# GFNet plus ReGLU on one core: half-height passes of the last 36 units in nine runs of eight, with the transforms' PSUM pair lent to the fourth unit

## The chip, the core and the metric

The kernel runs on one core of one Trainium2 chip. The metric is device time in microseconds (us) of one execution, shown as the median over several runs. The core has a matrix engine (TensorE, PE in the profile, with its weight loads as PEld), a vector engine (VectorE, DVE), a scalar engine (ScalarE, ACT), GpSimd (POOL) and SyncE (SP), which issues the transfers (its queue is SPq). Matmul results land in PSUM, which this kernel divides into eight banks of 128 partitions x 512 fp32 values.

## The reference

The output is the sum of the input, a two-dimensional Fourier filter (GFNet) of its layernorm, and a ReGLU MLP of the same layernorm. S = 2048 rows, D = 448 columns, F = 1792 hidden columns, everything fp32:

```
xn = layernorm(x)                                    # x: 2048 x 448
A  = irfft2(rfft2(xn) * (w_r + 1j * w_i), s=(S, D))  # w: 2048 x 225
g  = xn @ W_gate                                     # 448 x 1792
g  = g * (g > 0)
B  = (g * (xn @ W_up)) @ W_down                      # W_down: 1792 x 448
return x + A + B
```

## The kernel before

**MLP.** The rows are held transposed in four chunks of 512 (`CHUNKS`, index `q`, tiles `T`), the hidden columns in 14 slices of 128 (index `f`), in three groups of 5, 5 and 4 slices (`GROUPS`). One **unit** is one `f` for one `q`; there are 56. Every operand is split into a high and a low fp16 part, and three of the four products are kept. D = 448 is three and a half rows of 128, so a unit needs, for gate and for up each, ten full-height passes (`gu_full`, L757: 128 contraction rows, 512 columns) and one **half-height** pass (`gu_half`, L764: 64 rows). Gate and up of a unit each fill one PSUM bank. ScalarE then takes the ReLU of the gate (`gu_relu`, L799), VectorE multiplies by the up (`gu_times`, L803), and both split the product into fp16 halves `h` (`gu_hi`, L807; `gu_lo`, L811). These four are `gu_post`. When all units of a group are there for a chunk, four down passes (`dn_mm`, L834) of 12 or 15 matmuls each follow, and VectorE adds each result to the running output `xy` (`dn_post`, L840). The last four down passes of all are `dn_tail` (L853 matmuls, L857 VectorE), the last of them in two pieces of 336 and 112 columns.

**Runs of half passes.** Units are taken in sets: four sets of two, then sixteen of three. The first unit of a set does its full passes, and then the half passes of the whole set stand together (`gu_halves`), since changing between full and half height costs TensorE time. The other units of the set open their banks with their half pass; their full passes follow later.

**PSUM.** Six of the eight banks are three pairs for the units and the down passes (`banks`; those without an owner are in the list `idle`). The other two are a rotating pool tile `fx` with two buffers, for the transforms' matmuls.

**Transforms.** The Fourier work is a chain of small steps: `f_dft`, `f_eo`, `f_x`, `f_sdft`, `f_y1` forward, butterflies on VectorE, the filter, and then inverse. Per block of 128 rows (`n2`, sixteen) the inverse has the mirror-and-add steps `i_pair` and `i_quad` (with a transfer of mirrored rows, `sw`), `i_hi` (L632, ScalarE) and `i_lo` (L638, VectorE), `i_sdft` (L648, TensorE, 12 matmuls into `fx`), `i_pq` (L653, ScalarE) and `i_pqlo` (L657, VectorE), which read that bank, `i_ddft` (L667, TensorE, 12 matmuls into `fx`) and `i_acc` (L672, VectorE), which reads it. A single real row goes its own way (`row_dft` L593, `row_mul`, `row_ev`).

**Order.** The steps of the transforms stand in one list (`bg`), each with a VectorE cost, and a planner (`rooms`, `load`) gives each unit and each down pass a share of them. The program is recorded unit by unit, with priorities (`tc.high_priority`); a scheduler then fixes one order per engine. Each engine works through its own order and waits at an instruction whose inputs or bank are not ready.

Of the kernel before, what the change touches and what calls it, by code (L numbers as in the profile page):

```python
# [1 line left out]

# [18 lines left out]
GW = 2 * KC  # L21
# [3 lines left out]
LAG, AHEAD, RAMP = 1, 5, 8  # L25
NWARM = 21
# [118 lines left out]
def tile_gfnet_reglu(ctx: ExitStack, tc: tile.TileContext, x, xr, xi, wgu, wd, wf, c_fd, c_fm, c_im, c_row, c_id,  # L145
# [9 lines left out]

    def fx():
        return psum.tile([128, 512], F32, name="fx", bufs=2)
# [201 lines left out]
    zps, eo, X, Xh, yps, cur = {}, {}, {}, {}, {}, {}  # L359

    def f_dft(n2):
        q, j = n2 % 4, n2 // 4
        js = slice(128 * j, 128 * (j + 1))
        ps = fx()
        T = Tq[q]

        def mm(r, a, part, first=False):
            o = fd_off[part, r]
            P.matmul(ps[:, r * GW:(r + 1) * GW], T[:, a, js] if a < 8 else Tl[q][:, js], fd_t[:, o:o + GW],  # L369
                     start=first, stop=True, skip_group_check=True)  # L370
# [6 lines left out]
        zps[n2] = ps  # L377

    def f_eo(n2):
        ps = zps[n2]  # L380
        zc = ft([128, 2 * GW], F32, "zc", 2)
        A.activation(zc, ps[:, 2 * GW:4 * GW], AF.Copy, scale=2.0 ** -14)
# [3 lines left out]
        V.scalar_tensor_tensor(e2[:, 2 * GW:], ps[:, 0:2 * GW], 2.0 ** -14, zc, op0=OP.mult, op1=OP.subtract)  # L386
# [254 lines left out]
    def i_sdft(n2):  # L641
# [7 lines left out]
        sps[n2] = ps  # L649

    def i_pq(n2):
        pgh[n2] = it([GW, 2, 4, 128], F16, "pgh", 2)
        A.activation(pgh[n2][:, 0].rearrange("p a b -> p (a b)"), sps[n2][0:GW], AF.Copy, scale=2.0 ** -14)  # L653

    def i_pqlo(n2):
        hi, lo = (pgh[n2][:, h].rearrange("p a b -> p (a b)") for h in range(2))
        V.scalar_tensor_tensor(lo, sps[n2][0:GW], 2.0 ** -14, hi, op0=OP.mult, op1=OP.subtract)  # L657
# [3 lines left out]
    def i_ddft(n2):  # L661
# [7 lines left out]
        ips[n2] = ps  # L669

    def i_acc(n2):
        V.scalar_tensor_tensor(xy[:, n2, :], ips[n2][:, 0:D], fsc[:, 1:2], xy[:, n2, :], op0=OP.mult, op1=OP.add)  # L672
        store(n2)
# [94 lines left out]

    NOSYNC = mybir.DependencyInfo(mybir.DependencyClass.NoSync, mybir.DependencyReason.DATA)
    opened = set()  # L770

    def gu_unit(f, q, others):
# [22 lines left out]
    g1s = {}  # L795

# [415 lines left out]
    for i, u in list(enumerate(units))[START + 1:-4]:  # L1212
# [78 lines left out]
```

## Time and profile before

| | |
|---|---|
| time, median of 3 runs | 442.37 us (442.14 to 443.46) |
| the profiled execution | 443.54 us |
| its span, first to last instruction | 441.8 us |
| granted TensorE clock | 1.000 |
| busy PE | 435.3 us (99%) |
| busy DVE | 382.4 us (87%) |
| busy ACT | 184.6 us (42%) |
| busy POOL | 29.0 us (7%) |

In the rows of the profile, `L757` is a line of the kernel, `out<-in` the tiles by the program's names, and the shape that of one instruction. In a timeline a row has its start in us, its length, engine, line, operation and count (`x29`); instructions of one form that follow each other share a row. What ended an engine's idle time before the row stands in square brackets with its length. A matmul's own duration includes its way through the array, so that matmuls overlap; the cost of one is the pitch from start to start.

### The profile page before, as it was taken

The numbers are of one execution on the slowest core, as the hardware profiler recorded it, in microseconds if no ns is written. First come the engines' busy times: TensorE is split into PE (matmuls) and PEld (weight loads), VectorE is DVE, ScalarE is ACT, GpSimd is POOL, SyncE is SP. The second block draws the span as 40 slices with busy tenths as digits, with TensorE's granted clock in tenths as the row PEclk, the third lists the DMA queues.
The fourth block names the chain that finished last, engine by engine and source line by source line (L and its number), as shares of the span: only waits on it lengthen the run. The fifth ranks groups of instructions, "written<-read, shape, count | busy, mean of one in ns | idle before, by whom it ended". The sixth has DMA issues, their size and how long they took to land.

```text
span 441.8 us, 7428 instructions
## 1 busy us (share of the span) xinstructions
PE 435.3 (99%) x2641; PEld 221.5 (50%) x2641; DVE 382.4 (87%) x957; ACT 184.6 (42%) x396; POOL 29.0 (7%) x75
## 2 busy tenths in 40 slices
PE   8999999999999999999999999999999999999997
PEld 3743454454555544444545444444545556555664
DVE  6998677788996879999999999988997989798644
ACT  5995454274557327144023358233213232244220
POOL 3230020011100040000000020000000000000000
PEclk9999999999999999999999999999999999999999
DMA  7929899004021124242220210001111121210212
GB/s 244 322 75 213 267 357 216 23 1 97 23 86 58 45 68 129 84 127 85 85 85 1 84 42 2 0 1 42 43 43 49 48 98 30 74 56 33 77 63 104
DMA packets 37612, 39.54 MB, mean 90 GB/s; under 512 B 16534, under 2 KB 33352, under 8 KB 37576
## 3 DMA queue, kind: packets, MB, share of 16 engines
q1 hardware_dynamic: 37576, 39.09, 29.3%
q8 instruction: 20, 0.33, 0.3%
q14 instruction: 16, 0.13, 0.1%
HBM read 24.38 MB, written 3.67 MB: 64 GB/s over the span
## 4 chain that ended last, share of the span: by engine, by line
PE 90%; ACT 3%; DVE 2%; DMA 2%; issue 1%; SPq 1%; POOL 0%; ACTq 0%
PE bank L757 49%; PE bank L834 27%; PE bank L764 3%; PE fx L648 2%; PE fx L369 2%; PE fx L667 2%; PE fx L406 2%; PE bank L853 2%; DMA y<-in_xr 1%; DMA T<-tt 1%; ACT wt L699 1%; ACT junk L185 1%; ACT tt L304 1%; DVE wt L703 1%; DVE g L803 0%
## 5 line engine op out<-in xcount | busy, mean ns | idle before, releaser
L757 PE MATMUL bank<-T,wt 128*128 128x512 f16 (+1 forms) x1160 | 253.2, 372 | 1.8 <-DMA T<-tt 1.1
L757 PEld LDWEIGHTS <-wt 128*128 128x128 f16 x1160 | 110.9, 98 | 128.4 <-issue 7.2
L834 PE MATMUL bank<-wdt,h 128*128 128x448 f16 x624 | 122.6, 352 | 0.0
L834 PEld LDWEIGHTS <-h 128*128 128x128 f16 x624 | 60.6, 98 | 55.4
L807 ACT ACTIVATE h<-g 128x512 f16<-128x512 f32 x56 | 35.0, 627 | 77.2 <-DVE g L803 77.2
L799 ACT ACTIVATE g<-bank 128x512 f32<-128x512 f32 x56 | 33.2, 592 | 79.9 <-PE bank L757 43.8
L803 DVE SCALAR_TENSOR_TENSOR g<-bank,g 128x512 f32<-128x512 f32 x56 | 38.4, 685 | 10.8 <-PE bank L757 7.0
L811 DVE TENSOR_TENSOR h<-g,h 128x512 f16<-128x512 f32 x56 | 38.4, 686 | 10.3 <-ACT h L807 10.2
L840 DVE SCALAR_TENSOR_TENSOR xy<-bank,dsc,xy 128x448 f32<-128x448 f32 x44 | 29.9, 679 | 3.2 <-PE bank L834 2.9
L632 ACT ACTIVATE vt<-y,fsc 128x456 f16<-128x456 f32 x15 | 10.1, 674 | 34.5 <-issue 14.0
L699 ACT ACTIVATE wt<-wst,wsc 128x512 f16<-128x512 f32 x28 | 19.3, 714 | 11.7 <-DVE wsc L195 10.0
L703 DVE SCALAR_TENSOR_TENSOR wt<-wst,wsc,wt 128x512 f16<-128x512 f32 x28 | 20.4, 743 | 0.5 <-ACT wt L699 0.5
L188 POOL PARTITION_ALL_REDUCE wm<-wm x15 | 10.3, 686 | 152.1 <-ACT junk L185 117.6
L672 DVE SCALAR_TENSOR_TENSOR xy<-fx,fsc,xy 128x448 f32<-128x448 f32 x16 | 10.8, 681 | 10.9 <-PE fx L667 10.9
L185 ACT ACTIVATE junk<-wst 128x512 bf16<-128x512 f32 x28 | 17.2, 616 | 0.0
L764 PE MATMUL bank<-T,wt 64*128 64x512 f16 x112 | 15.6, 380 | 0.0
L397 ACT ACTIVATE Xh<-X 128x456 f16<-128x456 f32 x16 | 9.3, 579 | 13.0 <-DVE X L395 8.3
L648 PE MATMUL fx<-im,vt 128*128 128x128 f16 x192 | 13.3, 219 | 0.0
L667 PEld LDWEIGHTS <-pgh 114*128 114x128 f16 x192 | 10.9, 98 | 3.8 <-issue 0.8
L406 PE MATMUL fx<-Xh,fm 128*128 128x456 f16 x48 | 12.7, 356 | 0.0
L648 PEld LDWEIGHTS <-vt 128*128 128x128 f16 x192 | 11.6, 98 | 1.3
L667 PE MATMUL fx<-idc_t,pgh 114*128 114x112 f16 x192 | 12.1, 213 | 0.0
(168 smaller groups left out, 478.3 us busy)
## 6 DMA issues: line engine op xcount, KB each, us to landing
wst<-in_wgu SPq DMA_DIRECT2D x28, 256.0 KB
sw<-y SPq DMA_DIRECT2D x56, 112.2 KB
wf<-in_wf SPq DMA_DIRECT2D x16, 228.0 KB
xy<-in_x SPq DMA_DIRECT2D x16, 224.0 KB
y<-in_xr SPq DMA_DIRECT2D x15, 224.0 KB
out<-xy SPq DMA_DIRECT2D x15, 224.0 KB
wdst<-in_wd SPq DMA_DIRECT2D x14, 224.0 KB
fm<-in_c_fm SPq DMA_DIRECT2D x4, 256.0 KB
```

Of the source, the lines that this page charges most:

```text
L648: P.matmul(o, v[:, h, w], m[:, c, :], start=(i == 0), stop=(i == 2), skip_group_check=True)
L667: P.matmul(ps[:, o], h[:, a, i, :], idc_t[:, b, o], start=(j == 0), stop=(j == 2), skip_group_check=True)
L699: A.activation(w[:, 0:4, :], wst[f, g], AF.Copy, scale=wsc[f, g])
L703: V.scalar_tensor_tensor(w[:, 4:8, :], st, sc, w[:, 0:4, :], op0=OP.mult, op1=OP.subtract)
L757: last["P"] = P.matmul(hps[f, q][g][:, cs], wt[f, g][:, a, :], Tq[q][:, b, cs], start=(start and i == 0), stop=(stop and i == len(seq) - 1 ...
L764: m = P.matmul(hps[f, q][g][:, 0:512], wt[f, g][rows, 7, :], Tq[q][rows, b, :], start=start, stop=stop).ins
L799: last["A"] = A.activation(g1s[f, q], hps[f, q][0], AF.Relu, scale=2.0 ** -22).ins
L803: last["V"] = V.scalar_tensor_tensor(g1, hps[f, q][1], 2.0 ** -22, g1, op0=OP.mult, op1=OP.mult).ins
L807: A.activation(ht[f, q][:, 0, :], g1s[f, q], AF.Copy)
L811: V.tensor_tensor(h[:, 1, :], g1s.pop((f, q)), h[:, 0, :], op=OP.subtract)
L834: last["P"] = P.matmul(ps[:, 0:D], ht[f, q][:, a, js], wdt[f][:, b, :], start=(i == 0), stop=(i == n - 1)).ins
L840: last["V"] = V.scalar_tensor_tensor(xy[:, n2, :], dps[n2][:, 0:D], dsc[:, g:g + 1], xy[:, n2, :], op0=OP.mult, op1=OP.add).ins
```

## The change

The sets are four of two, four of three and nine of four (`RUNS`), so that the last 36 units' half passes stand in nine runs of eight where there were twelve of six. A set of four needs four bank pairs at once. The fourth is the transforms' pair: `fx` is no longer a rotating pool tile but two fixed banks, kept in `turn["pair"]`, which `fx()` takes in turn. In a run of eight one unit, for which no pair is idle, gets this pair. Its half passes come first in the run, and the first of them waits for the recorded readers of the pair (`seen`). The unit that closes with the run (the one whose full passes came before it) is read out at once (`gu_post` within `gu_halves`), and its pair becomes the transforms' pair. Before the set's first unit, `read_all` issues with a high priority all readers of the pair that are still outstanding (`f_eo`, `f_y1`, `row_mul`, `row_ev`, `i_pq`, `i_pqlo`, `i_acc`, each now issued once, by whoever comes first). Pending down passes now come before the last unit of a set rather than before its second. The number of matmuls of each kind and of the other engines' operations stays.

The diff, cut: the same bookkeeping of readers (`seen["fx"].append`, `reads`, `@reader`) is added to all functions named above and shown here for two of them.

```diff
+READ = 600
+RUNS = 4 * [3] + 9 * [4]
...
+    turn = {"pair": [psum.tile([128, 512], F32, name=f"fx{i}") for i in range(2)], "n": 0}
+
     def fx():
-        return psum.tile([128, 512], F32, name="fx", bufs=2)
+        turn["n"] += 1
+        return turn["pair"][turn["n"] % 2]
...
+    seen = {"fx": []}
+    unread, read = {}, set()
+
+    def reads(name, *fns):
+
+        for fn in fns:
+            unread[fn.__name__, name] = fn
+
+    def reader(fn):
+        @wraps(fn)
+        def once(*a):
+            key = fn.__name__, a
+            if key not in read:
+                read.add(key)
+                unread.pop(key, None)
+                fn(*a)
+        return once
+
+    def read_all():
+        for (_, a), fn in list(unread.items()):
+            fn(*a)
...
         sps[n2] = ps
-
+        reads((n2,), i_pq, i_pqlo)
+
...
+    @reader
     def i_pqlo(n2):
         hi, lo = (pgh[n2][:, h].rearrange("p a b -> p (a b)") for h in range(2))
-        V.scalar_tensor_tensor(lo, sps[n2][0:GW], 2.0 ** -14, hi, op0=OP.mult, op1=OP.subtract)
+        seen["fx"].append(V.scalar_tensor_tensor(lo, sps[n2][0:GW], 2.0 ** -14, hi, op0=OP.mult, op1=OP.subtract).ins)
...
         gu_open(f, q)
+        if len(others) > 2:
+            with tc.high_priority(offset=READ):
+                read_all()
         gu_full(f, q, gs, cs, True, False)
         gu_halves(f, q, *others)
...
         fresh = [u for u in others if u not in hps]
         for u in fresh:
-            gu_open(*u)
-        for i, u in enumerate((*others[::-1], (f, q))):
+            if idle:
+                gu_open(*u)
+            else:
+                hps[u] = turn["pair"]
+        lent = [u for u in fresh if hps[u] is turn["pair"]]
+        wait = seen["fx"] + [r for u in fresh for r in seen.get(id(hps[u]), [])] if lent else []
+        if lent:
+            seen["fx"] = []
+        order = lent + [u for u in (*others[::-1], (f, q)) if u not in lent]
+        for i, u in enumerate(order):
             for g in (1, 0):
                 with tc.high_priority(offset=2000 if i or not g else 0):
-                    m = gu_half(*u, g, u in fresh, m, i == len(others))
+                    m = gu_half(*u, g, u in fresh, m, u == (f, q))
+                    for r in wait:
+                        tc.add_manual_dep(m, r.name, SYNC, reason="half passes stand together")
+                    wait = []
         opened.update(others)
         gu_close(f, q)
+        if lent:
+            with tc.high_priority(offset=400):
+                gu_post(f, q)
+            posted.add((f, q))
+            turn["pair"] = idle.pop()
...
-    sets += [gseq[k:k + 3] for k in range(8, len(gseq), 3)]
+    k = 8
+    for n in RUNS:
+        sets.append(gseq[k:k + n])
+        k += n
...
-            if u == us[1] and pend and len(units) > START:
+            if u == us[-2 if len(us) > 2 else 1] and pend and len(units) > START:
...
-            with tc.high_priority(offset=400):
-                gu_post(f, q)
+            if (f, q) not in posted:
+                with tc.high_priority(offset=400):
+                    gu_post(f, q)
```

Functions move to other lines: `gu_full` from L757 to L796, `gu_half` from L764 to L803, `gu_relu` L799 to L859, `gu_times` L803 to L863, `gu_lo` L811 to L871, `i_sdft` L648 to L682, `i_pqlo` L657 to L694, `i_ddft` L667 to L704, `i_acc` L672 to L711, `i_lo` L638 to L672, `dn_tail` L853 and L857 to L915 and L919.

The order of instructions at three places follows, with the weight loads mostly left out; a row names the result's tile, its sources, and the semaphores that it waits for. First TensorE at the last run of half passes; `im` is the matrix of `i_sdft`, `T3` the transposed rows of the last chunk. Before:

```order
L667 MATMUL fx_4388<-idc_t_83,pgh_4275 128x112
L648 MATMUL fx_4401<-im_4193,vt1_2151 128x128 [waits PE_49]
...
L757 MATMUL bank2_113<-T3_65,wt_3117 128x512
...
L757 MATMUL bank3_114<-T3_65,wt_3120 128x512
...
L764 MATMUL bank1_112<-T3_65,wt_3305 128x512 [waits DVE_49]
L764 MATMUL bank0_111<-T3_65,wt_3302 128x512 [waits Activation_49]
L764 MATMUL bank5_116<-T3_65,wt_3249 128x512
L764 MATMUL bank4_115<-T3_65,wt_3246 128x512
L764 MATMUL bank3_114<-T3_65,wt_3120 128x512
L764 MATMUL bank2_113<-T3_65,wt_3117 128x512
```

And with the change:

```order
L682 MATMUL fx1_62<-im_4051,vt0_2122 128x128 [waits DVE_49]
...
L796 MATMUL bank3_116<-T3_67,wt_3035 128x512
...
L803 LDWEIGHTS wt_3174 [waits DVE_49]
L803 MATMUL fx1_62<-T3_67,wt_3174 128x512
...
L803 MATMUL fx0_61<-T3_67,wt_3171 128x512
...
L803 MATMUL bank1_114<-T3_67,wt_3127 128x512
...
L803 MATMUL bank0_113<-T3_67,wt_3124 128x512
...
L803 MATMUL bank3_116<-T3_67,wt_3035 128x512
...
L803 MATMUL bank2_115<-T3_67,wt_3032 128x512
```

Before, twelve `i_sdft` matmuls are followed by 14 full passes and a run of six into the three pairs. Now they are followed by eight full passes of the same unit and a run of eight, which starts in the bank (`fx1_62`) that the `i_sdft` has just written; the wait on VectorE stands on the weight load ahead of the first half pass.

That wait is for `i_pqlo` (L694) of this `i_sdft`. What VectorE has ahead of it with the change, from the multiply of the unit before on (`y3`, `y6`, `y7`, `y8` are blocks on their way through `i_pair` and `i_quad`; `sw2` holds mirrored rows):

```order
L863 SCALAR_TENSOR_TENSOR g1_4301<-bank1_114,g1_4301 128x512 [waits PE_49,Activation_49]
...
L711 SCALAR_TENSOR_TENSOR xy_63<-fx0_61,fsc_89,xy_63 128x448 [waits PE_49]
...
L655 TENSOR_TENSOR y7_75<-y7_75 128x228 [waits DVE_49]
L871 TENSOR_TENSOR h_4304<-g1_4301,h_4304 128x512 [waits Activation_49]
...
L584 TENSOR_TENSOR y6_74<-y6_74,sw2_2130 128x4x57 [waits DMAHW4_49,DMAHW3_49,DMAHW2_49]
L585 TENSOR_TENSOR y6_74<-y6_74,sw2_2130 128x4x57
...
L672 SCALAR_TENSOR_TENSOR vt0_2122<-y8_76,fsc_89,vt0_2122 128x456 [waits PE_49,Activation_49]
L694 SCALAR_TENSOR_TENSOR pgh_4297<-fx1_62,pgh_4297 114x512 [waits Activation_49]
```

Between that multiply and L694 stand thirteen operations. The last of them, L672, is the `i_lo` of a later block; it writes `vt0`, which this `i_sdft` reads, so it can't start ahead of that transform's end.

Last the end of TensorE's order. Before, and with the change:

```order
L667 MATMUL fx_4740<-idc_t_83,pgh_4706 128x112 [waits DVE_49]
...
L667 MATMUL fx_4754<-idc_t_83,pgh_4737 128x112 [waits DVE_49]
...
L853 MATMUL bank0_111<-wdt_3382,h_4430 128x336
...
L853 MATMUL fx_4824<-wdt_3382,h_4430 128x112 [waits DVE_49]
```

```order
L915 MATMUL fx0_61<-wdt_3387,h_4338 128x336
...
L704 MATMUL bank2_115<-idc_t_85,pgh_4643 128x112 [waits DVE_49]
...
L704 MATMUL bank3_116<-idc_t_85,pgh_4672 128x112 [waits DVE_49]
...
L915 MATMUL bank2_115<-wdt_3387,h_4338 128x112 [waits DVE_49]
```

The last two `i_ddft` (12 matmuls each) have moved from ahead of the 336-column piece to behind it, and the 112-column piece now shares its bank with the first of them. On VectorE the five operations at the end were L672, L672, L857 (448 columns), L857 (336), L857 (112) before, and are L711, L711, L919 (448), L919 (336), L919 (112) now.

More of the change, by code (lines that the diff above doesn't have):

```diff
@@ L1 @@
 from contextlib import ExitStack, contextmanager
+from functools import wraps
 import numpy as np
@@ L377, in f_dft @@
         zps[n2] = ps
+        reads((n2,), f_eo)
+    @reader
     def f_eo(n2):
@@ L381, in f_eo @@
         zc = ft([128, 2 * GW], F32, "zc", 2)
-        A.activation(zc, ps[:, 2 * GW:4 * GW], AF.Copy, scale=2.0 ** -14)
+        seen["fx"].append(A.activation(zc, ps[:, 2 * GW:4 * GW], AF.Copy, scale=2.0 ** -14).ins)
         e = eo[n2] = ft([128, 4, 2, KC], F32, "eo", 2)
@@ L385, in f_eo @@
         V.scalar_tensor_tensor(e2[:, 0:2 * GW], ps[:, 0:2 * GW], 2.0 ** -14, zc, op0=OP.mult, op1=OP.add)
-        V.scalar_tensor_tensor(e2[:, 2 * GW:], ps[:, 0:2 * GW], 2.0 ** -14, zc, op0=OP.mult, op1=OP.subtract)
+        seen["fx"].append(V.scalar_tensor_tensor(e2[:, 2 * GW:], ps[:, 0:2 * GW], 2.0 ** -14, zc, op0=OP.mult, op1=OP.subtract).ins)
     def f_x(n2):
@@ L406, in f_sdft @@
             P.matmul(y, m[:, a, :], xh[:, b], start=(i == 0), stop=(i == 2), skip_group_check=True)
+        reads((n2,), f_y1)
     def fresh(other):
@@ L444, in bfly @@
         return t, u
+    @reader
     def f_y1(n2):
@@ L448, in f_y1 @@
         if n2 < 8:
-            A.activation(t, yps[n2], AF.Copy)
+            seen["fx"].append(A.activation(t, yps[n2], AF.Copy).ins)
             cur["y", n2] = t
@@ L454, in f_y1 @@
             V.tensor_tensor(t, a, ps, op=OP.add)
-            V.tensor_tensor(u, a, ps, op=OP.subtract)
+            seen["fx"].append(V.tensor_tensor(u, a, ps, op=OP.subtract).ins)
             cur["s1", n2 - 8, 0], cur["s1", n2 - 8, 1] = t, u
@@ L593, in row_dft @@
             P.matmul(y, row_t[:, d, a], state["rowh"], start=(a == 0), stop=(a == 1), skip_group_check=True)
+        reads((), (row_mul, row_ev)[d])
+    @reader
     def row_mul():
@@ L601, in row_mul @@
         V.tensor_tensor(v, v, t, op=OP.add)
+    @reader
     def row_ev():
@@ L649, in i_sdft @@
         sps[n2] = ps
+        reads((n2,), i_pq, i_pqlo)
+    @reader
     def i_pq(n2):
         pgh[n2] = it([GW, 2, 4, 128], F16, "pgh", 2)
-        A.activation(pgh[n2][:, 0].rearrange("p a b -> p (a b)"), sps[n2][0:GW], AF.Copy, scale=2.0 ** -14)
+        seen["fx"].append(A.activation(pgh[n2][:, 0].rearrange("p a b -> p (a b)"), sps[n2][0:GW], AF.Copy, scale=2.0 ** -14).ins)
+    @reader
     def i_pqlo(n2):
         hi, lo = (pgh[n2][:, h].rearrange("p a b -> p (a b)") for h in range(2))
-        V.scalar_tensor_tensor(lo, sps[n2][0:GW], 2.0 ** -14, hi, op0=OP.mult, op1=OP.subtract)
+        seen["fx"].append(V.scalar_tensor_tensor(lo, sps[n2][0:GW], 2.0 ** -14, hi, op0=OP.mult, op1=OP.subtract).ins)
     ips = {}
@@ L669, in i_ddft @@
         ips[n2] = ps
+        reads((n2,), i_acc)
+    @reader
     def i_acc(n2):
-        V.scalar_tensor_tensor(xy[:, n2, :], ips[n2][:, 0:D], fsc[:, 1:2], xy[:, n2, :], op0=OP.mult, op1=OP.add)
+        seen["fx"].append(V.scalar_tensor_tensor(xy[:, n2, :], ips[n2][:, 0:D], fsc[:, 1:2], xy[:, n2, :], op0=OP.mult, op1=OP.add).ins)
         store(n2)
@@ L767, in gu_half @@
         return m
+    SYNC = mybir.DependencyInfo(mybir.DependencyClass.Sync, mybir.DependencyReason.DATA)
     NOSYNC = mybir.DependencyInfo(mybir.DependencyClass.NoSync, mybir.DependencyReason.DATA)
@@ L815, in gu_post @@
         gu_times(f, q)
+        seen[id(hps[f, q])] = [last["A"], last["V"]]
         gu_hi(f, q)
@@ L841, in dn_post @@
                                            op0=OP.mult, op1=OP.add).ins
+        seen[id(state["dn"])] = [last["V"]]
     def dn_tail(fs, ns):
```

1 line of the change is left out of this document (added).

## The prediction

> **What bounds the kernel now.** I read the page first, then who waited for whom on TensorE, then the timeline around single runs of half-height passes, and last the timeline of the end. Of the page:
>
> ```profile
> span 441.8 us, 7428 instructions
> ...
> PE 435.3 (99%) x2641; PEld 221.5 (50%) x2641; DVE 382.4 (87%) x957; ACT 184.6 (42%) x396; POOL 29.0 (7%) x75
> ```
>
> TensorE is busy for 435.3 of 441.8 us. A busy row alone proves little, so I asked what TensorE waited for after its first 40 us, and how busy the engines are in the middle (columns: PE, PEld, DVE, ACT, POOL, clock, DMA):
>
> ```profile
> PE bank L757 <- DMA T<-tt: 1.1, 1, 1.1
> ...
> 160.00:300.00 140.00, 140.00 (x696) 64.85 (x695) 136.00 (x318) 54.26 (x134) 9.95 (x19) 1.00 0.21 62
> ```
>
> One wait of 1.1 us is all. So what is taken out of TensorE's stream is gained in full, and a new wait in it is lost in full. VectorE is second, with 136.00 of 140 us between 160 and 300.
>
> **What a run costs, and what three fewer save.** The timeline (start, length, engine, line, count) around a run of six, and a run of four:
>
> ```profile
> 299.63 6.42 PE L757 MATMUL bank<-T,wt 128*128 128x512 f16 x29
> 305.98 0.82 PE L764 MATMUL bank<-T,wt 64*128 64x512 f16 x6
> 306.73 4.92 PE L757 MATMUL bank<-T,wt 128*128 128x512 f16 x22
> ...
> 46.02 0.61 PE L764 MATMUL bank<-T,wt 64*128 64x512 f16 x4
> ```
>
> A full pass comes every 0.216 us: (4.92 - 0.38) / 21, with the last one's 0.38 us length. The 29 before the run should take 6.25 us and take 6.35 from start to start, so entering a run costs 0.10. The six halves take 0.75 us to the next full pass, and 0.82 - 0.61 says that two more halves cost 0.21, a full pass, since the two run together. A run of six is thus 0.85 us and one of eight 1.06. The last 36 units now take 12 x 0.85 = 10.2 us and then 9 x 1.06 = 9.5: **0.65 us saved**. The number of full passes, transforms and down passes stays, and VectorE and ScalarE get the same operations in another order.
>
> **The wait at the head of the last run.** Lending the transforms' pair makes the first half pass wait for the pair's last reader. For seven of the nine runs no transform is near: the last reader is a unit's multiply or a row transform's, twenty passes (4.3 us) back, as far as the units' pairs were before. In the eighth the last `i_sdft` stands twenty passes ahead too. In the ninth only eight full passes lie between the last `i_sdft` and the run: from that transform's last pass, 0.06 + 8 x 0.216 = 1.79 us. What its readers take shows here (the fastest case, then the slowest):
>
> ```profile
> 414.92 0.83 PE L648 MATMUL fx<-im,vt 128*128 128x128 f16 x12
> 415.59 3.95 PE L834 MATMUL bank<-wdt,h 128*128 128x448 f16 x20
> 415.78 0.68 ACT L632 ACTIVATE vt<-y,fsc 128x456 f16<-128x456 f32 x1 [3.89 <-issue]
> 416.36 0.58 ACT L653 ACTIVATE pgh<-fx 114x512 f16<-114x512 f32 x1
> 416.49 0.69 DVE L638 SCALAR_TENSOR_TENSOR vt<-y,fsc,vt 128x456 f16<-128x456 f32 x1
> 417.10 0.68 DVE L657 SCALAR_TENSOR_TENSOR pgh<-fx,pgh 114x512 f16<-114x512 f32 x1
> ...
> 351.55 0.83 PE L648 MATMUL fx<-im,vt 128*128 128x128 f16 x12
> ...
> 356.31 0.68 DVE L657 SCALAR_TENSOR_TENSOR pgh<-fx,pgh 114x512 f16<-114x512 f32 x1
> ```
>
> The last transform pass starts 0.06 before 415.59, at 415.53; L657 ends at 417.78: 2.25 us. In the slow case it is 356.99 - 352.16 = 4.83. Against 1.79 the wait is at least 0.5 us (with 0.05 for the semaphore) and at most 3.1. Where between is decided by what stands before L657's successor (L694) on VectorE, and that order is fixed. I take its pitches, start to start, from:
>
> ```profile
> 377.74 0.69 DVE L638 SCALAR_TENSOR_TENSOR vt<-y,fsc,vt 128x456 f16<-128x456 f32 x1
> 378.35 0.39 DVE L621 TENSOR_TENSOR y<-y 128x228 f32<-128x228 f32 x1
> 378.65 0.68 DVE L657 SCALAR_TENSOR_TENSOR pgh<-fx,pgh 114x512 f16<-114x512 f32 x1
> 379.25 0.27 DVE L622 TENSOR_TENSOR y<-y 128x114 f32<-128x114 f32 x1
> 379.44 0.27 DVE L623 TENSOR_TENSOR y<-y 128x114 f32<-128x114 f32 x1
> ...
> 382.08 0.63 DVE L439 SCALAR_TENSOR_TENSOR y<-y,y 128x456 f32<-128x456 f32 x1
> 382.63 0.63 DVE L440 SCALAR_TENSOR_TENSOR y<-y,y 128x456 f32<-128x456 f32 x1
> ...
> 419.37 0.76 PE L667 MATMUL fx<-idc_t,pgh 114*128 114x112 f16 x12
> 419.96 0.83 PE L648 MATMUL fx<-im,vt 128*128 128x128 f16 x12
> 420.16 0.68 DVE L672 SCALAR_TENSOR_TENSOR xy<-fx,fsc,xy 128x448 f32<-128x448 f32 x1 [1.42 <-PE fx L667]
> ```
>
> The count starts at the `i_ddft` two before, whose `i_acc` VectorE waits for. From its first pass TensorE has: twelve passes (419.96 - 419.37 = 0.59), one down pass (0.19, as (3.95 - 0.35) / 19), `i_sdft` 0.67, twenty full 4.32, `i_ddft` 0.59, twelve full 2.59, `i_sdft` 0.67, eight full 1.73: the run stands at 11.35. VectorE starts `i_acc` at 0.79 (420.16 - 419.37). Up to L694 it has four rows of 448 at 0.59 (the tail below has that pitch), three of 512 at 0.60, two L638s at 0.61, two of 456 at 0.55, twelve of 228 at 0.30 and six of 114 at 0.19: 11.2. L694 starts at 12.0 and ends at 12.7: 1.4 us late. One operation in it, the pairing of `y6`, also waits for mirrored rows:
>
> ```profile
> 382.74 0.77 SPq L610 DMA_DIRECT2D y<-row  x1
> ...
> 384.34 0.70 SPq L548 DMA_DIRECT2D sw<-y  x1
> ...
> 182.58 0.72 SPq L548 DMA_DIRECT2D sw<-y  x1
> ...
> 185.17 0.40 DVE L553 TENSOR_TENSOR y<-y,sw 128x228 f32<-128x228 f32 x1 [0.60 <-DMA sw<-y]
> ```
>
> From the butterfly's end (6.5) to the data are 1.60 on SP's queue and 2.59 in flight: 10.7, where VectorE comes by at 10.4. So 1.4 to 1.7; I take **1.6 us lost**. Behind the waiting weight load stands all of TensorE's queue: seven halves, the next unit's passes, and with them ScalarE's ReLU and VectorE's multiply of the unit that closes. None has room to give it back.
>
> [...]
>
> **The end.** The inverse transforms now finish later in TensorE's order: the last two `i_ddft` stand behind the 336-column piece and right ahead of the 112-column one, which reuses the first one's bank and waits for its `i_acc`. Before:
>
> ```profile
> 435.04 1.34 PE L667 MATMUL fx<-idc_t,pgh 114*128 114x112 f16 x24
> 435.85 1.27 DVE L672 SCALAR_TENSOR_TENSOR xy<-fx,fsc,xy 128x448 f32<-128x448 f32 x2
> 436.23 1.88 PE L853 MATMUL bank<-wdt,h 128*128 128x336 f16 x12
> 437.94 0.75 PE L853 MATMUL fx<-wdt,h 128*128 128x112 f16 x12
> 438.14 0.57 DVE L857 SCALAR_TENSOR_TENSOR xy<-bank,dsc,xy 128x336 f32<-128x336 f32 x1 [0.43 <-PE bank L853]
> 438.73 0.33 DVE L857 SCALAR_TENSOR_TENSOR xy<-fx,dsc,xy 128x112 f32<-128x112 f32 x1
> ```
>
> From 435.04 VectorE ends at 439.06, 4.02 us later. Now the wide piece comes first (437.94 - 436.23 = 1.71), then the pair. The first `i_acc` starts 0.81 after its first pass (435.85 - 435.04), at 2.52, and ends at 3.20; TensorE would be there at 2.90 and waits 0.35. VectorE goes on, in order: the second `i_acc` at 3.11 (pitch 1.27 - 0.68 = 0.59), the 448-wide row at 3.70, the 336-wide at 4.29, the 112-wide at about 4.78 (its pitch estimated between those of 228 and 448), which ends at 5.11. That is **1.1 us lost** after the matmuls, where VectorE used to be free; 0.9 to 1.3 with the pitch unknown. The last `i_sdft`'s readers need 2.25 us and have 2.4 beside the wide piece, so they cost nothing; without that cover they would cost up to 2.3.
>
> The sum: 1.6 + 1.1 - 0.65 = +2.05 us. The profiled execution took 443.54 us around its 441.8 span, 1.2 above the median of the runs, 442.37; so 445.6 under the profiler and **444.4** as a median. What `read_all` and the earlier post of the closing unit move is on VectorE and ScalarE, under TensorE's passes; where that cover fails it is rival two.
>
> **Rivals.** *Not slower:* VectorE arrives at L694 unlate, as in 2.25 us. For it: its order is only bunched by 1.4 us, and the sum has 29 operations in it. Then the wait is 0.5 and the whole +0.95: 443.3, no difference that can be told, which here is 0.3%, 1.3 us. It decides from a wait under 0.9 us. Against it: the twelve 228-wide rows stand ahead in the order and cannot be passed.
>
> [...]
>
> *Slower still:* the saturated middle. There VectorE is close behind already:
>
> ```profile
> 201.74 0.68 DVE L803 SCALAR_TENSOR_TENSOR g<-bank,g 128x512 f32<-128x512 f32 x1
> ...
> 202.49 0.82 PE L764 MATMUL bank<-T,wt 64*128 64x512 f16 x6
> ```
>
> The bank was free at 202.42, 0.07 us before the run. If the new order puts half a microsecond more before the multiplies of the third and fourth long run, both wait: +1.0, in all 445.4. Against it: the distance of twenty passes is the same, and nine runs meet it instead of twelve.
>
> That the runs do not lengthen is ruled out by the order: seventeen runs, nine of them of eight.
>
> **Chances.** The forecast 0.64, with 443.7 to 445.0 its own; slower still 0.20; not slower 0.14; faster by over 0.3% 0.02, since even the whole saving without a wait is half of 1.3 us. Hence slower 0.82 (at 444.4 the change is +0.46%, and most of the two cases lies over 1.3), same 0.16, faster 0.02. The range, 443.2 to 446.0, goes from just under the first rival to the last run's wait at its upper bound without the rest.
>
> **What would show it.** In the changed profile: runs of eight of 1.03 us (0.82 + 0.21); TensorE's only new wait of over a microsecond at L803 for VectorE's L694, in the last run near 397 to 400; another of 0.3 to 0.4 at L915's last piece for L711; after the last matmul some 1.1 us of L711 and L919 on VectorE; a span near 443.9. The forecast is wrong if the last run starts without a wait, or if waits of half a microsecond stand at the runs between 200 and 300.

## The result, and the profile after

The change takes 447.01 us (median of 6 runs, 446.19 to 447.62) against 442.69 us (441.91 to 443.46, 6 runs) for the kernel before: ratio 1.0098, 95% interval 1.0086 to 1.0110. It is slower, as forecast, but by 4.3 us and not by 2.05, above the range of 443.2 to 446.0. The profiled execution has a span of 445.8 us at a granted clock of 1.000, 4.0 more than before.

What TensorE waited for after its first 40 us (engine, tile and line, what for, us in total, times, longest):

```profile
PE fx L803 <- DVE pgh L694: 2.3, 1, 2.3
PE bank L803 <- DVE g L863: 1.4, 1, 1.4
PE bank L796 <- DMA T<-tt: 0.5, 1, 0.5
PE bank L915 <- DVE xy L711: 0.2, 1, 0.2
```

The first row is the wait at the last run of eight, foreseen with 1.6 us. The last is the piece at the end, foreseen with 0.35. The second was only a rival: it is the third run of eight. The timeline there:

```profile
213.96 8.80 PE L796 MATMUL bank<-T,wt 128*128 128x512 f16 x40
...
218.80 0.38 DVE L632 SCALAR_TENSOR_TENSOR rowv<-bank,roww 48x228 f32<-48x228 f32 x1
...
221.32 0.38 DVE L634 TENSOR_TENSOR rowv<-rowv,rowm 48x228 f32<-48x228 f32 x1
...
223.37 0.69 DVE L863 SCALAR_TENSOR_TENSOR g<-bank,g 128x512 f32<-128x512 f32 x1
...
224.12 0.60 PE L803 MATMUL bank<-T,wt 64*128 64x512 f16 x4 [1.36 <-DVE g L863]
```

The first twenty of the 40 passes are a unit whose matmuls end at about 218.4 (213.96 + 19 x 0.216, and the last one's 0.38). VectorE multiplies it only at 223.37, 5 us later. The run, twenty passes on, needs that unit's bank at 222.7 and gets it at 224.1. The three operations of the real row (L632 to L634) stand ahead of the multiply, 5 us behind the matmuls that they read. In the kernel before they start 22 us behind theirs (216.52 us), when this run is long past:

```profile
238.14 0.38 DVE L599 SCALAR_TENSOR_TENSOR rowv<-fx,roww 48x228 f32<-48x228 f32 x1
```

`read_all` moved them, since they read a bank of the transforms' pair, which this run lends: with all sets of three, where it is never called, they start at 236.08 us.

At the last run:

```profile
391.78 0.63 DVE L470 SCALAR_TENSOR_TENSOR y<-y,y 128x456 f32<-128x456 f32 x1
...
392.71 1.24 SPq L578 DMA_DIRECT2D sw<-y  x1
...
394.00 0.70 SPq L579 DMA_DIRECT2D sw<-y  x1
...
394.27 0.83 PE L682 MATMUL fx<-im,vt 128*128 128x128 f16 x12
...
396.83 0.40 DVE L584 TENSOR_TENSOR y<-y,sw 128x228 f32<-128x228 f32 x1 [0.96 <-DMA sw<-y]
...
397.82 0.69 DVE L672 SCALAR_TENSOR_TENSOR vt<-y,fsc,vt 128x456 f16<-128x456 f32 x1
398.43 0.68 DVE L694 SCALAR_TENSOR_TENSOR pgh<-fx,pgh 114x512 f16<-114x512 f32 x1
...
399.17 0.39 PE L803 MATMUL fx<-T,wt 64*128 64x512 f16 x2 [2.34 <-DVE pgh L694]
```

VectorE stood still for 0.96 us for the mirrored rows of a later block and came to L694 1.60 us after they had landed. The end:

```profile
437.83 1.87 PE L915 MATMUL fx<-wdt,h 128*128 128x336 f16 x12
...
439.54 1.34 PE L704 MATMUL bank<-idc_t,pgh 114*128 114x112 f16 x24
440.33 1.28 DVE L711 SCALAR_TENSOR_TENSOR xy<-bank,fsc,xy 128x448 f32<-128x448 f32 x2 [0.98 <-PE bank L704]
441.07 0.75 PE L915 MATMUL bank<-wdt,h 128*128 128x112 f16 x12 [0.19 <-DVE xy L711]
...
442.60 0.32 DVE L919 SCALAR_TENSOR_TENSOR xy<-bank,dsc,xy 128x112 f32<-128x112 f32 x1
```

From the start of the 336-column piece to VectorE's end it takes 442.92 - 437.83 = 5.09 us.

**Where the 4 us are.** The two traces were laid side by side by their matmuls. From the run of half passes at 132 us (the last before any run of eight) to the start of the last matmul it is 306.00 us before and 309.55 with the change, 3.55 more. The waits there, as what the pitch exceeds its normal value by, are 2.41 (last run), 1.43 (third run) and 0.35 (end), 4.19 in sum. Three runs fewer take off 0.60: a run of six is 0.849 us with its entry, a run of eight 1.065, 12 x 0.849 - 9 x 1.065. That leaves 3.59, 0.04 over. Behind the last matmul VectorE's order adds 0.73 and the last transfer 0.24 (2.93 us from VectorE's end to the span's, 2.69 before). What comes before the first long run, 0.4 us less here, differs between executions of one kernel: the fourth run of half passes starts between 44.4 and 46.0 us in these profiles. The experiments are therefore read by their waits and, in places, by that stretch from 132 us on.

### The profile page after: what moved, and what is told of

It is laid out like the page before. It is cut to its first block, busy times and chain, and to the rows that moved or that the text cites. A ratio compares the mean times of both kernels' runs of the same rounds, so it can differ in the third digit from the quotient of the medians.

```text
span 445.8 us, 7415 instructions
## 1 busy us (share of the span) xinstructions
PE 435.1 (98%) x2641; PEld 222.1 (50%) x2641; DVE 382.4 (86%) x957; ACT 185.2 (42%) x396; POOL 30.9 (7%) x75
## 4 chain that ended last, share of the span: by engine, by line
PE 73%; DVE 13%; DMA 7%; ACT 3%; issue 2%; SPq 1%; POOL 0%; DVEq 0%; ACTq 0%
PE bank L796 32%; PE bank L895 18%; PE fx L796 7%; PE fx L895 4%; PE fx L396 2%; PE bank L803 2%; PE fx L435 2%; PE bank L682 2%; PE bank L915 2%; DMA sw<-y 1%; PE bank L704 1%; DVE g L863 1%; DMA xy<-in_x 1%; DVE xy L901 1%; ACT junk L191 1%
## 5 line engine op out<-in xcount | busy, mean ns | idle before, releaser
L796 PE MATMUL bank<-T,wt 128*128 128x512 f16 (+1 forms) x980 | 212.8, 370 | 1.2 <-DVE T L351 0.7
L796 PEld LDWEIGHTS <-wt 128*128 128x128 f16 x1160 | 111.0, 98 | 128.3 <-issue 6.8
L895 PE MATMUL bank<-wdt,h 128*128 128x448 f16 x510 | 101.2, 352 | 0.0
L859 ACT ACTIVATE g<-bank 128x512 f32<-128x512 f32 x47 | 27.7, 590 | 60.1 <-PE bank L796 32.2
L871 DVE TENSOR_TENSOR h<-g,h 128x512 f16<-128x512 f32 x56 | 38.3, 686 | 7.0 <-ACT h L867 6.9
L863 DVE SCALAR_TENSOR_TENSOR g<-bank,g 128x512 f32<-128x512 f32 x47 | 32.3, 686 | 11.2 <-PE bank L796 7.5
L796 PE MATMUL fx<-T,wt 128*128 128x512 f16 x180 | 40.5, 379 | 0.0
L901 DVE SCALAR_TENSOR_TENSOR xy<-bank,dsc,xy 128x448 f32<-128x448 f32 x36 | 24.5, 680 | 4.6 <-PE bank L895 4.5
L895 PE MATMUL fx<-wdt,h 128*128 128x448 f16 x114 | 22.4, 352 | 0.0
L803 PE MATMUL bank<-T,wt 64*128 64x512 f16 x94 | 13.7, 379 | 1.7 <-DVE g L863 1.7
L711 DVE SCALAR_TENSOR_TENSOR xy<-bank,fsc,xy 128x448 f32<-128x448 f32 x11 | 7.4, 681 | 8.7 <-PE bank L704 8.7
L770 ACT ACTIVATE wdt<-wdst,wds 128x448 f16<-128x448 f32 x14 | 9.1, 662 | 11.3 <-PE bank L895 4.4
L584 DVE TENSOR_TENSOR y<-y,sw 128x228 f32<-128x228 f32 x28 | 10.9, 389 | 2.0 <-DMA sw<-y 2.0
```

The source lines that it names most:

```text
L796: last["P"] = P.matmul(hps[f, q][g][:, cs], wt[f, g][:, a, :], Tq[q][:, b, cs], start=(start and i == 0), stop=(stop and i == len(seq) - 1 ...
L803: m = P.matmul(hps[f, q][g][:, 0:512], wt[f, g][rows, 7, :], Tq[q][rows, b, :], start=start, stop=stop).ins
L859: last["A"] = A.activation(g1s[f, q], hps[f, q][0], AF.Relu, scale=2.0 ** -22).ins
L863: last["V"] = V.scalar_tensor_tensor(g1, hps[f, q][1], 2.0 ** -22, g1, op0=OP.mult, op1=OP.mult).ins
L871: V.tensor_tensor(h[:, 1, :], g1s.pop((f, q)), h[:, 0, :], op=OP.subtract)
L895: last["P"] = P.matmul(ps[:, 0:D], ht[f, q][:, a, js], wdt[f][:, b, :], start=(i == 0), stop=(i == n - 1)).ins
```

## The experiments

### All sets of three: is the bookkeeping itself dear?

```diff
-RUNS = 4 * [3] + 9 * [4]
+RUNS = 16 * [3]
```

> All sets of three, so nothing is lent and no run of eight is left; the two fixed banks for the transforms and the readers' bookkeeping stay. Theory 'three places' (the loss of the change is the waits at the third and the last run of eight and the longer end): the time of before, ratio 0.999 to 1.001, and no wait of TensorE over 0.3 us at a run of half passes. Rival 'the fixed pair' (two fixed banks and the recorded readers order the transforms worse than the pool tile did): a part of the loss stays, ratio 1.002 to 1.006.

Ratio 1.0002 (0.9993 to 1.0010), no wait in the list, and the stretch takes 306.00 us. The fixed pair and the recorded readers cost nothing; all of the loss is with the sets of four.

### The last twelve units in sets of three

```diff
-RUNS = 4 * [3] + 9 * [4]
+RUNS = 4 * [3] + 6 * [4] + 4 * [3]
```

> Four sets of three, six of four, four of three: the last twelve units are as before, the six earlier runs of eight stay. Two runs fewer than before, 0.42 us. 'Three places': the wait of 2.3 us at the last run and the longer end (1.1 + 0.2 us) go, the 1.4 us at the third run stays, so 442.7 - 0.4 + 1.4 = 443.7 us, ratio 1.002, and a span 3.2 to 3.6 us under the 445.8 of the change. Rival 'VectorE is the bound' (a wait that is taken away comes back at the next place): the waits of TensorE stay at 3 to 4 us in sum, only elsewhere, ratio 1.007 to 1.010.

443.30 us, ratio 1.0019 (1.0010 to 1.0028), and one wait left after 50 us:

```profile
PE bank L803 <- DVE g L863: 1.2, 1, 1.2
```

The wait at the last run and the longer end go with the lending there, and neither comes back anywhere. The stretch is 306.84 us, 0.84 more than before: 1.25 of wait by the pitch, less 0.40 for two runs fewer. The rival fails for these two places.

### The real row later

```diff
-    rows = [lambda: (row_wf(), row_hi()), row_lo, lambda: row_dft(0), row_mul, row_hi2, row_lo2,
+    rows = [lambda: (row_wf(), row_hi()), row_lo, lambda: None, lambda: row_dft(0), row_mul, row_hi2, row_lo2,
...
-    rows_us = [0.0, 0.8, 0.0, 1.2, 0.0, 0.4, 0.0, 0.8]
+    rows_us = [0.0, 0.8, 0.0, 0.0, 1.2, 0.0, 0.4, 0.0, 0.8]
```

> The change, with the real row's first transform taken one step later in the list, so that its three reading multiplies stand behind the third run of eight and not ahead of it. 'Row first' (these three, 1.1 us of VectorE's order, stand ahead of the multiply that the third run waits for): that wait falls from 1.4 to 0.3 - 0.4 us, the last run's stays at 2.3, the time falls by 1.0 to 446.0 us, ratio 1.0075. Rival 'VectorE is the bound' (it has no idle time from 200 to 280 us, so it is late whatever stands first): the wait stays within 0.3 us of 1.4 or comes back at the fourth run, ratio 1.009 to 1.010.

447.05 us, ratio 1.0099 (1.0084 to 1.0115). The two runs, the third and the fourth of eight:

```profile
221.72 0.60 PE L803 MATMUL bank<-T,wt 64*128 64x512 f16 x4 [0.32 <-DVE g L863]
...
253.22 0.82 PE L803 MATMUL bank<-T,wt 64*128 64x512 f16 x6 [1.23 <-DVE g L863]
```

Both theories saw half. The third run's wait falls about as far as the three operations are long, to 0.39 us by the pitch. The fourth run, which now has the same three ahead of its multiply, waits 1.29, and a down pass at 235.4 us waits 0.31 for VectorE (too short an idle time for the list of waits). So they are what tipped the third run, but VectorE has no room for them at either place. The whole is no faster, as the rival had it.

### Both edits

```diff
-RUNS = 4 * [3] + 9 * [4]
+RUNS = 4 * [3] + 6 * [4] + 4 * [3]
...
-    rows = [lambda: (row_wf(), row_hi()), row_lo, lambda: row_dft(0), row_mul, row_hi2, row_lo2,
+    rows = [lambda: (row_wf(), row_hi()), row_lo, lambda: None, lambda: row_dft(0), row_mul, row_hi2, row_lo2,
```

> Both edits: sets 4 x 3, 6 x 4, 4 x 3, and the real row's first transform one step later. 'Three places': only 0.3 to 0.4 us of wait at the third run is left against 0.42 us saved by two runs fewer, so the time of before within 0.2 us, ratio 0.9995 to 1.0005. Rival 'VectorE is the bound': 1 us or more of waits at other runs, ratio over 1.0015.

444.34 us, ratio 1.0038 (1.0026 to 1.0051). The waits are those of the run above, by the pitch 0.36 and 1.29 us at the runs and 0.31 at the down pass. Less 0.40 for two runs fewer they make 1.56 us, and the stretch is 1.55 longer than before. The forecast of no difference was wrong for the same reason.

### VectorE relieved

```diff
-        last["V"] = V.scalar_tensor_tensor(xy[:, n2, :], dps[n2][:, 0:D], dsc[:, g:g + 1], xy[:, n2, :],
+        w = D if g == 0 else 64
+        last["V"] = V.scalar_tensor_tensor(xy[:, n2, 0:w], dps[n2][:, 0:w], dsc[:, g:g + 1], xy[:, n2, 0:w],
```

> The change, with VectorE relieved: the additions of the down passes of the second and third group take only the first 64 of 448 columns (the rest of these sums is left out), about 0.45 us less for each of 28. TensorE's work is the same. 'VectorE is late' (the third run waits because VectorE is 4.9 us behind there, where 3.6 are covered): the third run's wait goes and comes back at no other run; the last run's wait falls too, as the scheduler now puts 13 full passes and not eight between the last transform and the run: 0 to 1.0 us. Together 2.5 to 3.8 us less, 443.2 to 444.5 us. Rival 'the order of lending' (the waits come from what the lent unit has to wait for, whatever VectorE's load): both waits stay over 1 us, 445.5 us or more.

With most of these sums left out, the run tells something of the time alone. 444.29 us, ratio 1.0039 (1.0027 to 1.0052), inside what 'VectorE is late' expected, but not by the waits that it named:

```profile
PE fx L803 <- DVE pgh L694: 1.8, 1, 1.8
PE bank L803 <- DVE g L863: 0.9, 1, 0.9
```

The third run still waits 0.9 us: the scheduler fills the time that is freed ahead of the multiply with other work (VectorE is busy for 19.96 of the 20 us from 200 on). The fourth run's multiply is done 2.27 us ahead of it, against 0.52 in the change. At the last run the larger part of the wait has changed hands:

```profile
390.14 0.70 SPq L579 DMA_DIRECT2D sw<-y  x1
...
394.51 0.40 DVE L584 TENSOR_TENSOR y<-y,sw 128x228 f32<-128x228 f32 x1 [1.38 <-DMA sw<-y]
```

VectorE is earlier, and waits 1.38 us for the mirrored rows, which land 4.4 us after the second transfer's issue, where it was 2.8 in the change. The wait at the last run thus has two legs, VectorE's order and this transfer, and relieving the one shows the other.

### A bank of its own for the last piece

```diff
-        two = [(p, ns[3], c) for p, c in ((idle[2][0], slice(0, 3 * D // 4)), (fx(), slice(3 * D // 4, D)))]
+        two = [(p, ns[3], c) for p, c in ((idle[2][0], slice(0, 3 * D // 4)), (idle[2][1], slice(3 * D // 4, D)))]
```

> The change, with the last 112-column piece in a bank of a unit's pair that is free by then, so that it has no bank to wait for; eight of its 12 matmuls now stand ahead of the last two transforms. 'VectorE's order sets the end': TensorE's wait of 0.2 us there goes, VectorE's last five operations still follow each other, and from the start of the 336-column piece to VectorE's end it takes about 0.3 us longer than 5.09, since the last two transforms start 0.4 us later; the whole changes by less than 0.5 us, ratio 1.009 to 1.011. Rival 'the shared bank': the end is 0.5 to 1.1 us shorter, ratio 1.0073 to 1.0085.

447.74 us, ratio 1.0118 (1.0097 to 1.0140). TensorE's wait is gone and the end is longer all the same:

```profile
438.46 2.27 PE L915 MATMUL fx<-wdt,h 128*128 128x336 f16 x20
...
441.36 1.27 DVE L711 SCALAR_TENSOR_TENSOR xy<-bank,fsc,xy 128x448 f32<-128x448 f32 x2 [1.38 <-PE bank L704]
...
443.14 0.80 DVE L919 SCALAR_TENSOR_TENSOR xy<-fx,dsc,xy 128x336 f32<-128x336 f32 x2
```

443.94 - 438.46 = 5.48 us against 5.09: the last transforms start later, and VectorE's five operations follow them without a gap. The shared bank is not what makes the end longer. (The median is also lifted by two of the four executions, of 448.6 us, with a mean granted clock of 0.995 and 0.996; the other two, of 446.9, have 1.000 and 0.999. What lies behind that is shown below with the planner's credit.)

### Two other places for six runs of eight

```diff
-RUNS = 4 * [3] + 9 * [4]
+RUNS = 4 * [3] + [4, 3, 3, 4, 4, 4, 4, 4, 3, 3]
```

> Runs of eight only where the profile left room: the last 36 units in sets of 4, 3, 3, 4, 4, 4, 4, 4, 3, 3 (six of four), with runs of six through part of the stretch where VectorE is 3 to 5 us behind, and at the end. 'Three places': no wait over 0.5 us, 0.42 us saved, 442.0 us, ratio 0.999 to 1.000. 'VectorE is the bound': the real row's multiplies, which the first of the five long runs pulls ahead, cost 0.5 to 1.5 us at the next run of half passes, ratio 1.001 to 1.003.

442.95 us, ratio 1.0013 (1.0002 to 1.0024), with one wait of 0.7 us. And:

```diff
-RUNS = 4 * [3] + 9 * [4]
+RUNS = 4 * [3] + [3, 3, 4, 4, 4, 4, 4, 4, 3, 3]
```

> The same with sets of 3, 3, 4, 4, 4, 4, 4, 4, 3, 3. 'Three places': no wait over 0.5 us, 0.42 us saved, ratio 0.999 to 1.000. 'VectorE is the bound': a wait of 0.5 to 1.5 us at one of the runs between 200 and 260 us, ratio 1.001 to 1.003.

443.46 us, ratio 1.0022 (1.0012 to 1.0032), with one of 0.9 us. Both waits are for L863, at 231.8 us in both. This is what 'VectorE is the bound' expected, and not 'three places'. The real row's multiplies stand some thirty rows ahead of it in VectorE's order, outside the last unit before the run. So six runs of eight at other places still meet VectorE where it is late. That the real row is what makes it late there is not shown.

### The planner's credit, 2.5 us less through that stretch

`credit` is the planner's balance of VectorE time: while it is above zero, the next steps of the transforms' list are issued.

```diff
+            credit[0] += {39: -2.5, 61: 2.5}.get(i, 0.0)
             run_bg(amount=room[i] if i >= RAMP else 0.0)
```

> The change, with 2.5 us of VectorE's share of the transforms moved from ahead of the third and fourth run to behind them (the planner's credit is 2.5 us lower from unit 39 to unit 61); nothing is left out. 'VectorE is late': the third run's wait of 1.4 us falls under 0.4, no other of over 0.5 us comes up to 270 us, the last run's 2.0 to 2.4 us stay: 445.6 us, ratio 1.006 to 1.0075. Rival 'the order of lending': the third run still waits a microsecond, ratio 1.009 to 1.010.

No run but the last waits any more:

```profile
PE fx L803 <- DVE pgh L694: 2.5, 1, 2.5
```

Yet the time is 447.10 us, ratio 1.0092 (1.0069 to 1.0115), and not 445.6. The four executions are 445.14 us with a mean granted clock of 0.999, and 446.93, 447.26 and 447.35 with 0.996. The windows around the last run show where (columns: PE, PEld, DVE, ACT, POOL, clock, DMA):

```profile
396.00:398.00 2.00, 0.71 (x4) 0.28 (x6) 1.61 (x5) 0.00 (x0) 0.00 (x0) 0.80 0.17 58
398.00:400.00 2.00, 2.00 (x9) 0.49 (x6) 0.15 (x1) 0.60 (x1) 0.00 (x0) 0.50 0.00 0
400.00:402.00 2.00, 2.00 (x9) 0.84 (x8) 2.00 (x6) 0.63 (x1) 0.00 (x0) 0.84 0.00 0
```

Of the forecast the third run's wait was right, the whole time was not. The 2.5 us of wait end at 397.29, and the granted clock is lower by 0.20, 0.50 and 0.16 over these 2 us each, 1.7 us of full clock in sum. From the start of that run to the first pass of the next transform TensorE takes 7.32 us (397.29 to 404.61) where the change, at a clock of 1.00, takes 5.73 (399.17 to 404.90): 1.6 us lost beside the wait itself. In this order one run of eight was also broken into one and seven.

### The same credit with six runs of eight

```diff
-RUNS = 4 * [3] + 9 * [4]
+RUNS = 4 * [3] + 6 * [4] + 4 * [3]
...
+            credit[0] += {39: -2.5, 61: 2.5}.get(i, 0.0)
             run_bg(amount=room[i] if i >= RAMP else 0.0)
```

> Sets of 4 x 3, 6 x 4, 4 x 3 together with the credit of the run above. 'VectorE is late' with 'three places': no wait of over 0.4 us is left, and two runs fewer are saved, 0.42 us: 442.0 us, ratio 0.9985 to 0.9998, the only one under the kernel before. Rival: a wait of a microsecond somewhere else, ratio 1.001 to 1.003.

442.49 us, ratio 1.0001 (0.9992 to 1.0010). No wait is left, but the saving is missing too: the stretch takes 306.01 us. The broken run accounts for it:

```profile
221.69 0.39 PE L803 MATMUL bank<-T,wt 64*128 64x512 f16 x1
222.01 2.12 PE L796 MATMUL bank<-T,wt 128*128 128x512 f16 x9
224.06 0.60 PE L803 MATMUL bank<-T,wt 64*128 64x512 f16 x3
...
225.02 4.49 PE L796 MATMUL fx<-T,wt 128*128 128x512 f16 x20
```

One half pass stands alone, with nine full passes between it and the other seven, probably since the next one's bank still had the real row's result in it. The one takes 0.32 us to the next full pass and the seven 0.97, each with 0.10 for its entry: 1.48 us against 1.065 for a whole run. The 0.41 us between them is as much as the 0.40 that two runs fewer save.

### The last transform far from the last run, and near

```diff
+            credit[0] += {90: -3.0, 93: 3.0}.get(i, 0.0)
             run_bg(amount=room[i] if i >= RAMP else 0.0)
```

> The change, with the transforms' share held back by 3 us ahead of the last run of eight (credit, from unit 90 to 93): the last transform of the pair stands 40 full passes ahead of the run and not eight, and one more transform comes behind the 336-column piece at the end. 'The last transform's readers' (the last run waits for VectorE's L694 because only eight passes cover it): no wait at the last run, 2.3 us less there; at the end 12 transform matmuls more (0.67 us) and a new wait for their readers of about 1.6 us (2.25 us in the quickest case, less 0.6 of covering matmuls), so 447 us within 0.7. Rival 'VectorE is behind at the last run anyway': it waits a microsecond or more for its L863.

445.54 us, ratio 1.0070 (1.0054 to 1.0086), below the 447 within 0.7 that was expected. The last run does not wait, as 'the last transform's readers' had it; the third run's wait stays, and a smaller one than foreseen comes at the end:

```profile
PE bank L803 <- DVE g L863: 1.0, 1, 1.0
PE bank L704 <- DVE pgh L694: 0.6, 1, 0.6
```

With the signs turned round:

```diff
+            credit[0] += {90: 3.0, 93: -3.0}.get(i, 0.0)
             run_bg(amount=room[i] if i >= RAMP else 0.0)
```

> The opposite: the transforms' share is brought forward by 3 us, so that an i_sdft stands right ahead of the last run of eight, with no full pass between, and the last two i_ddft stand ahead of the 336-column piece as in the kernel before. 'The last transform's readers': the last run waits 2.2 us at least (the quickest case) and about 4.1 (what the change took from its last transform pass to L694's end), the end is 1.1 to 1.3 us shorter: 447.0 + 0.5 at most, 445.7 at least. Rival 'VectorE is behind anyway': the wait stays at 2.0 to 2.4 us with other readers named, 445.7 us.

448.44 us, ratio 1.0131 (1.0100 to 1.0162). The transform's matmuls now stand right ahead of the run:

```profile
398.15 0.83 PE L682 MATMUL fx<-im,vt 128*128 128x128 f16 x12 [0.84 <-DVE pgh L694]
400.33 0.68 DVE L694 SCALAR_TENSOR_TENSOR pgh<-fx,pgh 114x512 f16<-114x512 f32 x1
...
401.07 0.61 PE L803 MATMUL fx<-T,wt 64*128 64x512 f16 x2 [2.09 <-DVE pgh L694]
```

From the last transform pass (398.15 + 0.62) to L694's end it is 2.24 us, the quickest case of the prediction; in the change it was 4.22 (394.27 + 0.62 to 399.11), with the transfer in it. The wait is not longer without a cover, as the estimate of 4.1 us had it, because VectorE's order moved along: no mirrored rows are waited for between the transform and L694. A second wait of 0.84 us stands ahead of the transform, and in the profiled execution the granted clock is 0.55 from 400 to 402 us, where the longer one ends, and the eight full passes from 402.89 on take 3.60 us where 1.89 are usual (7 x 0.216 + 0.38), so that this time holds more than the waits. So the last run waits for the pair's last reader when a transform is near, and does not when it is far.

### 3.5 us less credit, and no broken run

```diff
-RUNS = 4 * [3] + 9 * [4]
+RUNS = 4 * [3] + 6 * [4] + 4 * [3]
...
+            credit[0] += {39: -3.5, 61: 3.5}.get(i, 0.0)
             run_bg(amount=room[i] if i >= RAMP else 0.0)
```

> As the run with sets of 4 x 3, 6 x 4, 4 x 3 and lowered credit, but 3.5 us in place of 2.5: the real row's matmuls now stand elsewhere, and no run of eight is broken in two. 'A broken run cost it': from the run of half passes at about 132 us to TensorE's last matmul 306.0 - 0.42 = 305.6 us (the kernel before: 306.00), no wait over 0.3 us, about 442.05 us, ratio 0.9985 to 0.9997. Rival 'lending itself costs 0.4 us somewhere': 306.0 again, ratio 0.9995 to 1.0007.

441.89 us against 442.32 for the kernel before, ratio 0.9991 (0.9982 to 1.0000). The stretch takes 305.58 us, 0.42 less than before, where two runs fewer save 0.40. The third run of eight just makes it:

```profile
221.42 0.69 DVE L863 SCALAR_TENSOR_TENSOR g<-bank,g 128x512 f32<-128x512 f32 x1
...
222.20 0.61 PE L803 MATMUL bank<-T,wt 64*128 64x512 f16 x4
```

The multiply ends at 222.11, 0.09 us ahead of the run. This is the only version ahead of both kernels, by 0.1%, at the edge of what its interval can tell from nothing. The difference to the 306.01 above, 0.43 us, is what the broken run cost there by its rows (0.41), though that order differs in other rows too.

And the change itself with the same credit, all nine runs of eight whole:

> The change with the credit lowered by 3.5 us from unit 39 to 61, all nine runs of eight whole. 'VectorE is late': the third run waits 0 to 0.3 us, the last 2.0 to 2.5 us as before, and from the run at about 132 us to TensorE's last matmul it takes 306.0 - 0.65 + 2.3 + 0.2 = 307.9 us at full clock (the change: 309.55); about 445.4 us, more where TensorE's granted clock falls behind the long wait. Rival 'the order of lending': over 309 us.

```profile
PE fx L803 <- DVE pgh L694: 2.0, 1, 2.0
```

444.78 us, ratio 1.0062 (1.0041 to 1.0082), and 307.76 us for the stretch where 307.9 was expected. The third run's wait was VectorE's lateness: with 3.5 us of its work, the real row among it, moved behind that stretch, where it has room, the wait is gone and comes back at no other run.

## Why the prediction was wrong

- **TensorE bounds, and a wait is lost in full.** Right. In the change the stretch from 132 us on is the work before, less what three runs fewer save, plus the waits, to 0.04 us. The same sum fits to 0.04 us with all sets of three (306.00) and with 3.5 us less credit (305.58 and 307.76).
- **What three fewer runs save: 0.65.** Right within 0.05 (0.60).
- **The wait at the last run: 1.6.** The place, the reader and the mechanism were right, the size was not: 2.41 by the pitch. The term that failed is the one of the mirrored rows. The text put the butterfly's end at 6.5 on its scale, but by its own pitches the last operation only starts there (6.42) and ends at 7.05; the trace has 7.09 (392.41 - 385.32). With that slip the data were expected at 10.7, only 0.3 behind VectorE. They came at 11.51, where VectorE stood ready at 10.55. The slip is 0.55 of the missing 0.8 us, and 0.23 is that the rows took 4.42 us from the butterfly's end and not 4.19. From L694's end to the first half pass, put at 0.05 for the semaphore, it is 0.06 (399.11 to 399.17).
- **Seven of nine runs have no transform near, and twenty passes cover the rest.** This is the step that failed most, with 1.43 us at the third run. It was kept as the rival of the saturated middle, at 0.20 and +1.0 us for two runs, from a row of that stretch (0.07 us of room), and set aside with the argument that the distance stays the same. The distance did stay; VectorE's lateness did not. The run of six that stood nearest in time to the third run of eight, before:

```profile
219.55 8.37 PE L757 MATMUL bank<-T,wt 128*128 128x512 f16 x38
...
226.68 0.69 DVE L803 SCALAR_TENSOR_TENSOR g<-bank,g 128x512 f32<-128x512 f32 x1
...
227.85 0.82 PE L764 MATMUL bank<-T,wt 64*128 64x512 f16 x6
```

  There the unit's last 18 passes end at about 223.6, and its multiply follows 3 us later, not 5. Of the difference 1.1 us is the real row, which `read_all` moved and which the prediction put down as covered work ("under TensorE's passes", and as this rival where that fails). The rest, about 0.8 us of the 1.9 between 0.48 us of room there and 1.43 us of wait here, lies in how the scheduler set the other operations, and no single one was found for it. VectorE has no time to absorb either: in the change it is busy for

```profile
200.00:220.00 20.00, 20.00 (x102) 9.86 (x101) 19.95 (x48) 5.46 (x16) 0.00 (x0) 1.00 0.28 87
...
280.00:300.00 20.00, 20.00 (x102) 9.88 (x101) 16.96 (x48) 3.40 (x6) 0.80 (x1) 1.00 0.00 1
```

  19.95 of 20 us there, and 16.96 eighty microseconds on, where the experiments with the credit moved the work.
- **The end: 1.1.** Right: 5.09 us against the 5.11 worked out, with 0.35 us of TensorE's wait in it. The 0.24 us of SyncE's last transfers behind VectorE were not in the sum.
- **The rivals.** 'Not slower' is out. 'Slower still' came at the third run alone, with 1.43 us where it had half a microsecond each at the third and the fourth. The lent pair itself was waited for at one of nine runs, 2.3 us at the last, as the sum had it; lending it shows a saving, 0.42 us with six runs of eight, only once the readers' lateness is taken out of its way.

By the corrected terms the sum is 2.41 + 1.43 + 0.35 + 0.73 + 0.24 - 0.60 = 4.56 us, against 4.3 between the medians and 4.0 between the two profiled spans, whose first 46 us differ by 0.4.

## What to carry to other kernels

A bank that is lent needs not only its own readers early: whatever is issued early for it stands ahead of something else on an engine's order, and on an engine that is busy for 19.95 of 20 us the next thing on the critical path pays. So before a buffer is taken from one user for another, look up for each place how late its last reader runs, and not only how far away it stands, and take it where that lateness leaves room: of nine places here seven cost nothing, and the other two cost six times what all nine saved. Where a wait hangs on a chain, add its pitches up once more: half a microsecond of a sum was a fifth of this forecast's error (0.55 of 2.6 us).

## What the runs showed of the hardware

In some profiles here TensorE's granted clock is 0.50 over a window of 2 us behind a wait of 2 to 2.5 us in the middle of dense work, and in others with such a wait it stays at 1.00. In the profile of the 2.5 us credit, shown above, it is 0.50 from 398 to 400 us (0.80 and 0.84 in the windows around it), behind a wait of 2.5 us that ends at 397.29. With a wait of 2.0 us at the last run it is 0.50 from 400 to 402 us in the profiles with the real row later (0.65 in the window before) and with a bank of its own for the last piece (0.78), where the waits end at 398.24 and 398.12. In that of the change with 3.5 us less credit, where such a wait ends at 396.43, it is 1.00 from 394 to 402. The change's own six timed executions, with a wait of 2.3 us in the profiled one, are all at 1.000:

```profile
396.00:398.00 2.00, 0.83 (x4) 0.20 (x2) 1.17 (x5) 0.29 (x1) 0.00 (x0) 1.00 0.33 102
398.00:400.00 2.00, 0.83 (x8) 0.31 (x8) 1.48 (x4) 0.00 (x0) 0.00 (x0) 1.00 0.17 57
```

These are the windows of the change around its wait, which ends at 399.17. From the start of the last run to the first pass of the next transform (8 half passes and 22 full ones) TensorE takes 5.73 us in the change and with 3.5 us less credit, and 7.32, 7.37 and 7.40 with the 2.5 us credit, with the real row later and with a bank of its own for the last piece. The executions of the 2.5 us credit run are 445.1 us with a mean granted clock of 0.999 and 1.8 to 2.2 us longer with 0.996. A lower mean does not always come with a longer time: with 3.5 us less credit one execution has 444.69 us at 0.997, beside 444.61 and 444.88 at 1.000 and 446.79 at 0.996. What decides whether the clock falls is not shown. So a wait of this length cost itself in some executions and some 2 us more in others, and a median over few runs can show either.
